# Weights of the second layer converted during the first and parked in DRAM, seven block products in its first group, and a sum kept in PSUM

## The chip, the cores and the metric

The kernel runs on one core of a Trainium2 chip. The metric is device time in microseconds (us) of one execution. Three runs of the kernel before took 1055.42, 1055.51 and 1057.75 us, so the median is 1055.51 us. Work is spread over TensorE (PE; PEld is its loading of weights), VectorE (DVE), ScalarE (ACT) and the DMA queue that SyncE (SP) feeds.

## The reference, cut to what matters

Attention between channels (its scores are 256 x 256), and then two feed-forward layers over 6016 tokens, 256 wide, with 2048 hidden features. The first layer has ELU between its two products, the second SiLU.

```python
def reference(...):
    attn_out = _attn_ref(**attn_kwargs)          # v @ softmax(kn^T qn / tau), (1, 6016, 256)
    x = attn_out.reshape(6016, 256)
    x = _moe_ref(x, w_in, w_out)                 # ELU
    return _moe2_ref(x, w_in2, w_out2)           # SiLU

def _moe_ref(x, w_in, w_out):
    h = x @ w_in                                 # 256 -> 2048
    g = np.where(h > 0.0, h, np.exp(np.minimum(h, 0.0)) - 1.0)
    return (g @ w_out).astype(np.float32)        # 2048 -> 256

def _moe2_ref(x, w_in, w_out):
    h = x @ w_in
    g = h * (1.0 / (1.0 + np.exp(-h)))
    return (g @ w_out).astype(np.float32)
```

## The kernel before, in words

The attention matrix is folded into the first layer's input weights (`m_group`), so that the two layers are the bulk. Tokens go in six groups of 1024 (the last has 896). `order` (line 642) lists twelve stretches, a layer and a group each: layer 1 on groups 0 to 5, then layer 2 on groups 0, 5, 1, 2, 3, 4. A stretch has eight steps j, one for each pair of 128 hidden features (16 pieces of 128 in all).

Every number in a product is carried as two float32r parts, a high and a low one, and a `product` (line 263) is three matmuls of up to 512 columns. `split` (line 259) makes the two parts: an ACT copy for the high one and a DVE subtraction for the low one.

The first product of a step is a 2 x 2 block product: two feature pieces by two halves of the tokens, over two halves of the 256 inputs. In a *plain* stretch (lines 648 and 740; here group 0 of both layers) it takes eight block products. In the others it takes seven, by sums of weight blocks (S1 to S4, `weight_sums`) and of inputs (T1 to T4, `x_made`). `first_a` (line 758) does four of them into the four PSUM banks x, y, w, z; ACT copies x to `u` in SBUF, and DVE adds u += y, v = w + u, v += z; v is the hidden value (1,1). `first_b` (line 777) lets three more products accumulate on x, w and z; x is the value (0,0), and DVE adds w + u and z + u give the other two in SBUF. So there are five adds a step. A `unit` (line 723) takes each hidden value through the activation: Relu and Exp on ACT and a scalar_tensor_tensor on DVE for ELU, two Silu on ACT for SiLU, and the split into `gs`. `second` (line 796) multiplies `gs` by the output weights `wo` into the four y banks.

The weights come as 64-bit numbers, and `convert` (line 378) makes two parts of them: load to a 4 KB buffer `st` (three in a ring), two ACT passes, two DVE tensor_scalar, a scalar_tensor_tensor and an integer add, and the split. The second layer's w2i also needs four 128x128 weight sums and a second split. Before the change, layer 2's weights are converted while layer 2's group 0 runs (lines 912 and 917), one piece of w2i and one of w2o in each of its eight steps, straight into `wa`, `a21` and `wo` that layer 1 has left by then. In this stretch only the four plain weight blocks are needed at once.

The order: all operations are recorded, and `in_order` (line 70) puts them out by a list schedule with the costs of line 36. PE's order is that of the program; ACT, DVE and SP get what is ready, the longest remaining way first. Engines then run their queues strictly in that order.

Of the kernel before, what the change touches and what calls it, by code (L numbers as in the profile page):

```python
# [11 lines left out]
F32 = mybir.dt.float32  # L12
F32R = mybir.dt.float32r
# [3 lines left out]
ALU = mybir.AluOpType  # L17
AX = mybir.AxisListType

P = 128  # L20
# [119 lines left out]
def channel_attention_elu_silu(  # L140
# [29 lines left out]
    _, N, C = q.shape  # L170
# [24 lines left out]
    small = one.tile([P, 224], F32, tag="small", name="small")  # L195
    wide = one.tile([P, GJ + 2 * MJ, C], F32, tag="wa", name="wide")
    v0 = wide[:, :GJ]
    wo = [one.tile([P, NF, C], F32R, tag=f"wo{a}", name=f"wo{a}") for a in range(2)]
    a21 = one.tile([P, 2, NP, P], F32R, tag="a21", name="a21")
    y_ps = [ps.tile([P, FC], F32, tag=f"y{i}", name=f"y{i}") for i in range(4)]  # L200
    h_ps = [ps.tile([P, FC], F32, tag=f"h{i}", name=f"h{i}") for i in range(4)]
    y_dram = [dram.tile([P, CT, GJ * P], F32, tag=f"yd{i}", name=f"yd{i}") for i in range(NG)]

    def f32(ap):
        return ap.bitcast(F32)
# [31 lines left out]
    def copy(out, src, **kw):  # L237
        act(out, src, AF.Copy, **kw)

    def tt(out, a, b, op):  # L240
        do("DVE", width(out.ap), lambda: nc.vector.tensor_tensor(at(out), at(a), at(b), op), [a, b], [out])  # L241
# [17 lines left out]
    def split(hi, lo, src):  # L259
        copy(hi, src)  # L260
        tt(lo, src, V(f32(hi.ap), hi.keys), ALU.subtract)
# [44 lines left out]
    def part(v, ap, *what):  # L306
        return V(ap, tuple(v.keys[0]._replace(what=x) for x in what))

    def cols_of(v, n):
        return V(v.ap[:, :n], v.keys)  # L310
# [15 lines left out]
    def wa_at(part, j, a):  # L326

        jj = range(j.start, j.stop) if isinstance(j, slice) else [j]
        aa = range(a.start, a.stop) if isinstance(a, slice) else [a]
        return V(wa[:, part, j, a], tuple(("wa", part, x, y) for x in jj for y in aa))  # L330

    def a21_at(part, j):
        jj = range(j.start, j.stop) if isinstance(j, slice) else [j]
        return V(a21[:, part, j], tuple(("a21", part, x) for x in jj))
# [21 lines left out]
    def load(name, i, *order):  # L356
        src = weights[name].rearrange("(t p) f -> p t f", p=P)
        src = src[:, :, 2 * i * HC : 2 * (i + 1) * HC] if name[-1] == "i" else src[:, 2 * i : 2 * i + 2]
        a, b = src.shape[1], src.shape[2]
        t = sts.take()  # L360
        words = t.ap.bitcast(I32)
        dma(V(words.rearrange("p (a b) -> p a b", a=a), t.keys + order), V(src, ()))
        words = words.rearrange("p (a b w) -> p a b w", a=a, w=2)
        src_of[name, i] = [part(t, words[:, :, :, w], w) for w in range(2)]

    def flat(ap):
        return ap.rearrange("p a b -> p (a b)")

    def weight_sums(s, w0, w1):

        get = lambda v, i: V(v.ap[:, :, i], v.keys)
        put = lambda i: part(s, s.ap[:, :, i], i)
        tt(put(0), get(w0, 1), get(w1, 1), ALU.add)
        tt(put(1), get(w0, 0), put(0), ALU.subtract)
        tt(put(2), get(w0, 0), get(w0, 1), ALU.subtract)
        tt(put(3), get(w1, 0), put(1), ALU.add)

    def convert(name, i, *order):
        load(name, i, *order)
        low, high = src_of.pop((name, i))  # L380
        t = cvs.take()
        a, b = low.ap.shape[1:3]
        w = V(t.ap.rearrange("p (a b) -> p a b", a=a), t.keys)
        wi = V(w.ap.bitcast(I32), t.keys)
        copy(w, V(f32(high.ap), high.keys), scale=2.0**-112)
        copy(low, V(low.ap.bitcast(U32), low.keys), scale=2.0**-29)
        ts(w, w, TOP, -TOP, ALU.min, ALU.max)
        ts(wi, wi, 3, None, ALU.logical_shift_left)
        stt(wi, V(high.ap, high.keys), SIGN, wi, ALU.bitwise_and, ALU.bitwise_or)
        tt(V(flat(wi.ap), wi.keys), V(flat(wi.ap), wi.keys), V(flat(low.ap), low.keys), ALU.add)  # L390
        if name == "w1i":
            s = slice(i % 2 * HC, (i % 2 + 1) * HC)
            hi, lo = (w1i_at(i // 2, a, slice(None)) for a in range(2))
            pieces = [(V(hi.ap[:, :, s], hi.keys), V(lo.ap[:, :, s], lo.keys), w)]
        elif name[-1] == "o":
            pieces = [(wo_at(0, i), wo_at(1, i), w)]
        else:
            pieces = [
                (wa_at(0, i, A11), wa_at(1, i, A11), V(w.ap[:, 0, :P], w.keys)),
                (a21_at(0, i), a21_at(1, i), V(w.ap[:, 0, P:], w.keys)),  # L400
                (
                    *(wa_at(a, i, slice(A12, A22 + 1)) for a in range(2)),
                    V(w.ap[:, 1].rearrange("p (a b) -> p a b", a=2), w.keys),
                ),
            ]
        for hi, _, src in pieces:
            copy(hi, src)
        for hi, lo, src in pieces:
            tt(lo, src, V(f32(hi.ap), hi.keys), ALU.subtract)
        if name == "w2i":  # L410
            h = hs.take()
            s = V(h.ap.rearrange("p (j a b) -> p j a b", j=1, a=4), h.keys)
            two = lambda c: V(w.ap[:, c].rearrange("p (j a b) -> p j a b", j=1, a=2), w.keys)
            weight_sums(s, two(0), two(1))
            split(*(wa_at(a, i, slice(S1, S4 + 1)) for a in range(2)), V(s.ap[:, 0], s.keys))

    with tc.manual_schedule():
        make_identity(nc, ident)
# [226 lines left out]
        def cols(n):  # L645
            return groups[order[n][1]][1] * P // 2

        def plain(n):

            return order[n][1] == 0  # L650

        base = [0] * len(order)
        for n in range(1, len(order)):
# [99 lines left out]
                )  # L753
            unit(s, u, ps)

        banks, us = {}, {}

        def first_a(s):
            n, j = steps[s]
            m = cols(n)  # L760
            if plain(n):
                for u in UNITS[:2]:
                    first_plain(s, u)
                return
            b = banks[s] = [cols_of(bank(), m) for _ in range(4)]
            for ps, a, o in zip(b, (A11, S2, S3, S1), (B11, T2, T3, T1)):
                product(ps, pair(j, a), x_at(n, o))
            x, y, w, z = b
            u, v = (cols_of(hs.take(), m) for _ in range(2))
            us[s] = u  # L770
            copy(u, x)
            tt(u, y, u, ALU.add)
            tt(v, w, u, ALU.add)
            tt(v, z, v, ALU.add)
            unit(s, (1, 1), v)

        def first_b(s):
            n, j = steps[s]
            if plain(n):
                for u in UNITS[2:]:  # L780
                    first_plain(s, u)
                return
            (x, _, w, z), u = banks.pop(s), us.pop(s)
            for ps, a, o in ((x, A12, B21), (w, A22, T4), (z, S4, B22)):
                product(ps, pair(j, a), x_at(n, o), start=False, skip_group_check=True)
            unit(s, (0, 0), x)
            t = cols_of(hs.take(), cols(n))
            tt(t, w, u, ALU.add)
            unit(s, (1, 0), t)
            tt(u, z, u, ALU.add)  # L790
            unit(s, (0, 1), u)


        final = len(order) - 1
# [107 lines left out]
        for s in range(len(steps) + 1):  # L902
            prev = s - 1
            now = s < len(steps)
            if now:
                n, j = steps[s]
                if n and j == 0:
                    x_made(n)
                if n == 0 and j % 2 and j < NP - 1:
                    convert("w1i", j + 1)  # L910
                    convert("w1i", j + 2)
                if order[n] == (2, 0):
                    convert("w2i", j)
                first_a(s)
            if s:
                chunk = f"w{order[steps[prev][0]][0]}o", steps[prev][1]
                if plain(steps[prev][0]) and chunk not in EARLY:
                    convert(*chunk)
                second(prev, (1, 1))
                if now:  # L920
                    second(prev, (1, 0))
            if now:
                if n == 0 and j % 2 and j < NP - 1:
                    m_group(j // 2 + 1)
                first_b(s)
            if s:
                second(prev, (0, 1))
                if not now:
                    y_store_final(1)
                    second(prev, (1, 0))  # L930
                second(prev, (0, 0))
                if steps[prev][1] == NP - 1:
                    if steps[prev][0] == final:
                        y_store_final(0)
                    else:
                        y_store(steps[prev][0])
# [36 lines left out]
```

## Time and profile before

| | |
|---|---|
| median of three runs | 1055.51 us |
| the profiled execution, first to last instruction | 1055.5 us |
| PE busy | 1042.7 us (99%) |
| DVE busy | 848.9 us (80%) |
| ACT busy | 716.0 us (68%) |
| granted TensorE clock, mean | 0.997 |
| DMA traffic | 54.60 MB |

The profiled execution has no time outside its span that the run's time would show: both are 1055.5. The first 62 us are the attention's scores; then come the twelve stretches, layer 1 from 62.7 us to about 560 us, layer 2 to 1050 us. An instruction's own time in a row is its latency; instructions of one engine overlap a little, so the distance from start to start (the pitch) is what one costs a full engine. Line numbers of the profile are those of the code above.

### The profile page before, as it was taken

Reading aid. Unit: us, or ns where it says so; the run is one execution under the profiler, and the core shown is the slowest. Engines: PE = TensorE matmul, PEld = TensorE weight load, DVE = VectorE, ACT = ScalarE, POOL = GpSimd, SP = SyncE. Lnnn points to the kernel's source line nnn. Section 1 sums busy time; section 2 is a strip of 40 time slices with the busy share of each in tenths; the row PEclk is TensorE's granted clock in tenths of the full one; section 3 lists DMA queues with packets and bytes.
Section 4 is the critical chain, followed back from the end, with each engine's and each line's share of the span. In section 5 each row is a group of like instructions: output and inputs, shape, how many; then the busy total and the mean of one; then the engine's idle time right before and its main releaser. Section 6 shows DMA issues by size and latency. Waiting matters only on the chain.

```text
span 1055.5 us, 13381 instructions
## 1 busy us (share of the span) xinstructions
PE 1042.7 (99%) x4848; PEld 882.5 (84%) x4848; DVE 848.9 (80%) x1432; ACT 716.0 (68%) x1304; POOL 0.8 (0%) x7
## 2 busy tenths in 40 slices
PE   8999999999999999999999999999999999999998
PEld 7778888888888888888998888998888888888997
DVE  6899999999989989989989966667668668657554
ACT  5699988786777777777879845555556455455543
POOL 0000000000000000000000000000000000000000
PEclk9999999999999999999999999999999999999999
DMA  9932241112003003002004303003003003001101
GB/s 348 286 94 60 81 98 62 41 21 60 1 6 74 1 1 75 1 1 80 20 1 140 110 1 75 6 1 76 1 1 80 0 1 80 1 1 23 18 1 40
DMA packets 99602, 54.60 MB, mean 52 GB/s; under 512 B 83024, under 2 KB 84304, under 8 KB 98896
## 3 DMA queue, kind: packets, MB, share of 16 engines
q1 hardware_dynamic: 99440, 53.49, 18.3%
q8 instruction: 38, 0.62, 0.2%
q10 hardware_dynamic: 96, 0.26, 0.1%
q14 instruction: 28, 0.23, 0.1%
HBM read 41.42 MB, written 12.32 MB: 51 GB/s over the span
## 4 chain that ended last, share of the span: by engine, by line
PE 93%; DMA 4%; DVE 1%; SPq 0%; ACT 0%; issue 0%; DVEq 0%
PE y L268 49%; PE h L268 44%; DMA ring<-in_q_dram 2%; DMA wide<-in_q_dram 1%; DMA wide<-in_v_dram 1%; DMA st<-in_moe_w_out_dram 0%; SPq L257 0%; DVE wo L241 0%; DVE cv L247 0%; DVE xs L241 0%; PE h L281 0%; DVE cv L241 0%; PE y L281 0%; PE h L276 0%; DVE cv L244 0%
## 5 line engine op out<-in xcount | busy, mean ns | idle before, releaser
L268 PE MATMUL y<-gs,wo 128*128 128x512 f32 (+1 forms) x2112 | 500.0, 386 | 0.7 <-DVE gs L241 0.7
L268 PE MATMUL h<-xs,wa 128*128 128x512 f32 (+1 forms) x1968 | 472.9, 386 | 0.0
L268 PEld LDWEIGHTS y<-gs,wo 128*128 128x128 f32 x2112 | 395.9, 188 | 76.2 <-DVE e L850 2.7
L268 PEld LDWEIGHTS h<-xs,wa 128*128 128x128 f32 x1968 | 368.0, 188 | 69.4 <-DVE h L241 2.0
L241 DVE TENSOR_TENSOR h<-h,h 128x512 f32<-128x512 f32 (+1 forms) x400 | 269.9, 675 | 78.5 <-PE h L268 69.1
L241 DVE TENSOR_TENSOR gs<-e,gs 128x512 fp32r<-128x512 f32 (+1 forms) x384 | 257.8, 677 | 71.0 <-ACT e L233 67.5
L233 ACT ACTIVATE e<-h 128x512 f32<-128x512 f32 (+2 forms) x385 | 229.8, 600 | 71.7 <-DVE h L241 48.3
L233 ACT ACTIVATE gs<-h 128x512 fp32r<-128x512 f32 (+1 forms) x192 | 117.0, 609 | 159.7 <-DVE h L241 109.8
L247 DVE SCALAR_TENSOR_TENSOR e<-e,h 128x512 f32<-128x512 f32 (+1 forms) x192 | 128.5, 676 | 26.2 <-ACT e L233 25.8
L233 ACT ACTIVATE gs<-e 128x512 fp32r<-128x512 f32 (+1 forms) x192 | 116.6, 614 | 23.0 <-DVE e L247 22.7
L233 ACT ACTIVATE e<-e 128x512 f32<-128x512 f32 (+1 forms) x192 | 117.2, 616 | 2.4
L233 ACT ACTIVATE h<-h 128x512 f32<-128x512 f32 (+1 forms) x80 | 46.3, 579 | 37.4 <-PE h L268 37.1
L241 DVE TENSOR_TENSOR xs<-big,xs 128x512 fp32r<-128x512 f32 (+1 forms) x74 | 48.7, 676 | 2.2 <-ACT xs L233 2.2
L268 PEld LDWEIGHTS y<-wo,gs 128*128 128x128 f32 x384 | 47.9, 192 | 1.1
L268 PE MATMUL y<-wo,gs 128*128 128x256 f32 x384 | 48.3, 283 | 0.0
L233 ACT ACTIVATE xs<-big 128x512 fp32r<-128x512 f32 (+1 forms) x74 | 43.1, 614 | 3.4 <-PE h L268 2.3
L241 DVE TENSOR_TENSOR sums<-sums 128x2048 f32<-128x2048 f32 (+2 forms) x16 | 28.7, 1792 | 10.4 <-ACT sums L233 10.2
L268 PE MATMUL h<-xs,a 128*128 128x512 f32 x96 | 27.3, 392 | 1.1 <-ACT a L233 1.1
L244 DVE TENSOR_SCALAR cv<-cv 128x512 f32<-128x512 f32 (+1 forms) x64 | 26.4, 430 | 1.3 <-ACT cv L233 1.3
L233 ACT ACTIVATE cv<-st 128x512 f32<-128x512 f32 x32 | 21.3, 671 | 7.6 <-DVE h L241 3.2
L276 PE MATMUL y<-ring 128*128 128x256 f32 x92 | 23.6, 415 | 1.7 <-DMA ring<-in_k_dram 1.7
L276 PEld LDWEIGHTS y<-ring 128*128 128x128 f32 x92 | 18.6, 207 | 5.7 <-issue 2.3
(84 smaller groups left out, 376.1 us busy)
## 6 DMA issues: line engine op xcount, KB each, us to landing
st<-in_moe_w_in_dram SPq DMA_DIRECT2D x16, 512.0 KB, 3.8
st<-in_moe_w_out_dram SPq DMA_DIRECT2D x16, 512.0 KB, 3.7
yd<-e SPq DMA_DIRECT2D x20, 256.0 KB, 2.5
big<-yd SPq DMA_DIRECT2D x5, 1024.0 KB, 4.7
out_dram<-big SPq DMA_DIRECT2D x38, 128.0 KB, 2.9
big<-in_v_dram SPq DMA_DIRECT2D x32, 128.0 KB, 3.4
wide<-in_q_dram SPq DMA_DIRECT2D x6, 512.0 KB, 10.0
wide<-in_k_dram SPq DMA_DIRECT2D x6, 512.0 KB, 10.7
```

The source lines that it names most:

```text
L233: nc.scalar.activation(at(out), at(src), func, **{k: at(x) for k, x in kw.items()}, **more)
L241: do("DVE", width(out.ap), lambda: nc.vector.tensor_tensor(at(out), at(a), at(b), op), [a, b], [out])
L244: do("DVE", width(out.ap) / 2, lambda: nc.vector.tensor_scalar(at(out), at(a), at(s1), at(s2), *op), [a, s1, s2], [out])
L247: emit = lambda: nc.vector.scalar_tensor_tensor(at(out), at(a), at(s), at(b), op0, op1)
L268: nc.tensor.matmul(at(out), at(lhs[a]), at(rhs[b]), start=start and a + b == 0, stop=stop and a == 1, **kw)
L276: emit = lambda: nc.tensor.matmul(at(out), at(lhs), at(rhs), start=start, stop=stop, **kw)
```

## The change

Three things. Layer 2's weights are converted by a new `put_by` in the steps of layer 1's groups 1 to 4 (four pieces in each group), each written to DRAM in its final two parts, sums of blocks included; `take_back` loads piece j into `wa` and `wo` when step j of layer 1's last group has read the old one. Then group 0 of layer 2 is no longer plain: `plain` is true for the first stretch alone. And `first_a` adds u to w and z in their PSUM banks before `first_b` accumulates on them, so that the three other values are read from PSUM; ACT makes a second copy (v from z), and DVE has four adds a step where it had five.

```diff
+    wo_both = one.tile([P, 2, NF, C], F32R, tag="wo", name="wo")
+    wo = [wo_both[:, a] for a in range(2)]
+    wa_dram = [dram.tile([P, 2, 7, P], F32, tag=f"wad{i}", name=f"wad{i}") for i in range(NP)]
+    wo_dram = [dram.tile([P, 2, 2, C], F32, tag=f"wod{i}", name=f"wod{i}") for i in range(NP)]
...
+    def put_by(name, i):
+        w, raw = in_f32(name, i)      # load, two ACT passes, four DVE operations, as in convert
+        wf = V(flat(w.ap), w.keys)
+        both = V(raw.ap.rearrange("p (a x) -> p a x", a=2), raw.keys)
...
+        split(half(both, 0), half(both, 1), wf)
+        if name == "w2o":
+            dma(V(wo_dram[i].rearrange("p a x r -> p a (x r)"), (("wod", i),)), both)
+            return
+        dma(V(wa_dram[i][:, :, A11], (("wad", i, 0),)), V(blocks(both)[:, :, 0], both.keys))
+        dma(V(wa_dram[i][:, :, A12 : A22 + 1], (("wad", i, 1),)), V(blocks(both)[:, :, 2:], both.keys))
+        t, more = cvs.take(), sts.take()
...
+        weight_sums(V(t.ap.rearrange("p (j a b) -> p j a b", j=1, a=4), t.keys), two(0), two(1))
+        both = V(more.ap.rearrange("p (a x) -> p a x", a=2), more.keys)
+        split(half(both, 0), half(both, 1), t)
+        dma(V(wa_dram[i][:, :, S1:], (("wad", i, 2),)), V(blocks(both), both.keys))
+
+    def take_back(name, i):
+        if name == "w2o":
+            keys = tuple(k for a in range(2) for k in wo_at(a, i).keys)
+            dma(V(f32(wo_both[:, :, 2 * i : 2 * i + 2]), keys), V(wo_dram[i], (("wod", i),)))
+        else:
+            keys = tuple(k for a in range(2) for k in wa_at(a, i, slice(0, 7)).keys)
+            dma(V(f32(wa[:, :, i]), keys), V(wa_dram[i], tuple(("wad", i, x) for x in range(3))))
...
         def plain(n):
-            return order[n][1] == 0
+            return n == 0
...
             u, v = (cols_of(hs.take(), m) for _ in range(2))
-            us[s] = u
             copy(u, x)
+            copy(v, z)
             tt(u, y, u, ALU.add)
-            tt(v, w, u, ALU.add)
-            tt(v, z, v, ALU.add)
+            tt(w, w, u, ALU.add)
+            tt(v, w, v, ALU.add)
+            tt(z, z, u, ALU.add)
             unit(s, (1, 1), v)
...
-            unit(s, (0, 0), x)
-            t = cols_of(hs.take(), cols(n))
-            tt(t, w, u, ALU.add)
-            unit(s, (1, 0), t)
-            tt(u, z, u, ALU.add)
-            unit(s, (0, 1), u)
+            for u, ps in zip(((0, 0), (1, 0), (0, 1)), (x, w, z)):
+                unit(s, u, ps)
...
-                if order[n] == (2, 0):
-                    convert("w2i", j)
+                if 0 < n < NG - 1 and j % 2 == 0:
+                    at_ = ((n - 1) * NP + j) // 2
+                    put_by(("w2i", "w2o")[at_ % 2], at_ // 2)
...
+                if steps[prev][0] == NG - 1:
+                    take_back("w2i", steps[prev][1])
+                    take_back("w2o", steps[prev][1])
```

PE's queue in layer 2, group 0: `y` are the banks of the second product, `h` those of the first, and a row's `x6` counts matmuls. A second product's half (12 matmuls) and the first product's second half that follows it, before:

```order
L268 MATMUL y2_72<-gs_291,wo0_67 128x512 x2
L268 MATMUL y2_72<-gs_291,wo1_68 128x512
L268 MATMUL y3_73<-gs_291,wo0_67 128x512 x2
L268 MATMUL y3_73<-gs_291,wo1_68 128x512
L268 MATMUL y0_70<-gs_291,wo0_67 128x512 x2
L268 MATMUL y0_70<-gs_291,wo1_68 128x512
L268 MATMUL y1_71<-gs_291,wo0_67 128x512 x2
L268 MATMUL y1_71<-gs_291,wo1_68 128x512
L268 MATMUL h2_76<-xs_345,a21_69 128x512 x3
L268 MATMUL h2_76<-xs_345,wa_376 128x512 x3
L268 MATMUL h3_77<-xs_345,a21_69 128x512 x3
L268 MATMUL h3_77<-xs_345,wa_376 128x512 x3
```

The same place of PE's queue now (lines are 3 higher, and the two parts of `wo` have one name):

```order
L271 MATMUL y2_71<-gs_306,wo_67 128x512 x3
L271 MATMUL y3_72<-gs_306,wo_67 128x512 x3
L271 MATMUL y0_69<-gs_306,wo_67 128x512 x3
L271 MATMUL y1_70<-gs_306,wo_67 128x512 x3
L271 MATMUL h2_75<-xs_360,wa_391 128x512 x3
L271 MATMUL h0_73<-xs_360,wa_391 128x512 x3
L271 MATMUL h1_74<-xs_360,wa_391 128x512 x3
```

The first product's half of 12 matmuls became one of 9; the other half keeps its 12, and the second product its 24.

DVE's queue in layer 1, group 2, from the fourth step's first add on (`h0_74` and `h1_75` are the banks w and z, `h1_97` is u, `h2_98` is v, `big` and `xs` belong to the next group's inputs), before:

```order
L241 TENSOR_TENSOR h1_97<-h3_77,h1_97 128x512
L247 SCALAR_TENSOR_TENSOR e2_94<-e2_94,h3_99 128x512
L241 TENSOR_TENSOR h2_98<-h0_74,h1_97 128x512
L241 TENSOR_TENSOR big0_84<-big1_85 128x512
L241 TENSOR_TENSOR h2_98<-h1_75,h2_98 128x512
L241 TENSOR_TENSOR gs_291<-e2_94,gs_291 128x512
L241 TENSOR_TENSOR xs_345<-big1_85,xs_345 128x512
L247 SCALAR_TENSOR_TENSOR e3_95<-e3_95,h2_98 128x512
L241 TENSOR_TENSOR h3_99<-h0_74,h1_97 128x512
L247 SCALAR_TENSOR_TENSOR e0_92<-e0_92,h2_76 128x512
L241 TENSOR_TENSOR h1_97<-h1_75,h1_97 128x512
```

The same step of DVE's queue now (`h0_73` and `h1_74` are w and z, `h0_111` is u, `h1_112` is v, `cv` and `st` are pieces of layer 2's weights):

```order
L244 TENSOR_TENSOR h0_111<-h3_76,h0_111 128x512
L244 TENSOR_TENSOR gs_306<-e2_109,gs_306 128x512
L244 TENSOR_TENSOR h0_73<-h0_73,h0_111 128x512
L244 TENSOR_TENSOR h1_74<-h1_74,h0_111 128x512
L244 TENSOR_TENSOR h1_112<-h0_73,h1_112 128x512
L244 TENSOR_TENSOR gs_306<-e0_107,gs_306 128x512
L244 TENSOR_TENSOR cv2_106<-cv1_105 128x128 x2
L244 TENSOR_TENSOR cv2_106<-cv1_105,cv2_106 128x128
L244 TENSOR_TENSOR st2_103<-cv1_105,st2_103 128x512
L250 SCALAR_TENSOR_TENSOR e3_110<-e3_110,h1_112 128x512
L244 TENSOR_TENSOR cv2_106<-cv1_105,cv2_106 128x128
L247 TENSOR_SCALAR cv0_104<-cv0_104 128x512
```

All four adds stand together near the step's head, w and z are written in place, and where the first list goes on with adds, conversions stand between v and the operation that reads it. DVE's queue has the conversions from the end of group 0 to the end of group 4 of layer 1, with some in every step.

## Rows read from the trace of the kernel before

**Rows 1.** The page, part 1: busy us, share, instructions.

```profile
PE 1042.7 (99%) x4848; PEld 882.5 (84%) x4848; DVE 848.9 (80%) x1432; ACT 716.0 (68%) x1304; POOL 0.8 (0%) x7
```

**Rows 2.** The page, part 2: tenths busy in 40 slices.

```profile
DVE  6899999999989989989989966667668668657554
...
PEclk9999999999999999999999999999999999999999
```

**Rows 3.** Windows: busy us (records) per engine, clock, DMA share, GB/s.

```profile
75.00:166.00 91.00, 91.00 (x404) 75.40 (x403) 90.95 (x166) 85.66 (x157) 0.00 (x0) 1.00 0.30 80
...
248.00:330.00 82.00, 82.00 (x361) 67.27 (x360) 74.33 (x120) 61.74 (x114) 0.00 (x0) 1.00 0.12 26
...
560.00:647.00 87.00, 87.00 (x389) 72.64 (x388) 70.00 (x152) 61.52 (x126) 0.00 (x0) 1.00 0.28 88
807.00:889.00 82.00, 82.00 (x363) 67.91 (x363) 56.82 (x89) 44.75 (x80) 0.00 (x0) 1.00 0.11 26
```

**Rows 4.** Chain of waits in time order: start us, us, what.

```profile
248.83 2.99 PE y L268 x12
251.83 2.20 PE h L268 x9
254.03 2.75 PE y L268 x12
...
588.21 2.72 PE h L268 x12
```

**Rows 5.** Lines of DVE, 248 to 330 us, shapes apart.

```profile
L241 DVE TENSOR_TENSOR h<-h,h 128x512 f32<-128x512 f32 x40 | 27.4, 686 | 1.6 <-PE h L268 1.2
...
L251 DVE STREAM_TRANSPOSE big<-big 128x1024 f32<-128x1024 f32 x2 | 2.5, 1238 | 0.0
```

**Rows 6.** Timeline of DVE, four places: start us, us, instruction.

```profile
84.42 0.68 DVE L241 CUSTOM_DVE_ANT_0 cv<-st,cv 128x1024 uint16<-128x1024 uint16 x1
85.02 0.69 DVE L241 TENSOR_TENSOR gs<-e,gs 128x512 fp32r<-128x512 f32 x1
85.62 0.69 DVE L247 SCALAR_TENSOR_TENSOR cv<-st,cv 128x512 int32<-128x512 int32 x1
...
90.76 0.43 DVE L244 TENSOR_SCALAR cv<-cv 128x512 f32<-128x512 f32 x1
91.09 1.25 DVE L251 STREAM_TRANSPOSE big<-big 128x1024 f32<-128x1024 f32 x1
...
261.16 0.69 DVE L241 TENSOR_TENSOR h<-h,h 128x512 f32<-128x512 f32 x1
261.76 0.69 DVE L241 TENSOR_TENSOR big<-big 128x512 f32<-128x512 f32 x1
...
562.21 0.28 DVE L241 TENSOR_TENSOR h<-cv,h 128x128 f32<-128x128 f32 x1
562.41 0.69 DVE L247 SCALAR_TENSOR_TENSOR cv<-st,cv 128x512 int32<-128x512 int32 x1
```

**Rows 7.** Timeline of a step, 288 to 294 us, ACT, DVE and PE.

```profile
288.20 0.58 ACT L233 ACTIVATE h<-h 128x512 f32<-128x512 f32 x1
...
289.02 1.48 DVE L241 TENSOR_TENSOR h<-h,h 128x512 f32<-128x512 f32 x2
...
291.01 0.68 DVE L241 TENSOR_TENSOR h<-h,h 128x512 f32<-128x512 f32 x1
293.06 0.69 DVE L247 SCALAR_TENSOR_TENSOR e<-e,h 128x512 f32<-128x512 f32 x1 [1.36 <-ACT e L233]
...
292.66 2.20 PE L268 MATMUL h<-xs,wa 128*128 128x512 f32 x9
```

**Rows 8.** Waits, and DMA issues with KB and us to landing.

```profile
ACT cv L233 <- DMA st<-in_moe_w_out_dram: 2.3, 2, 1.3
...
st<-in_moe_w_out_dram SPq DMA_DIRECT2D x16, 512.0 KB, 3.7
big<-yd SPq DMA_DIRECT2D x5, 1024.0 KB, 4.7
```

More of the change, by code (lines that the diff above doesn't have):

```diff
@@ L197, in channel_attention_elu_silu @@
     v0 = wide[:, :GJ]
-    wo = [one.tile([P, NF, C], F32R, tag=f"wo{a}", name=f"wo{a}") for a in range(2)]
+    wo_both = one.tile([P, 2, NF, C], F32R, tag="wo", name="wo")
+    wo = [wo_both[:, a] for a in range(2)]
     a21 = one.tile([P, 2, NP, P], F32R, tag="a21", name="a21")
@@ L364, in load @@
         src_of[name, i] = [part(t, words[:, :, :, w], w) for w in range(2)]
+        return t
     def flat(ap):
@@ L376, in weight_sums, with in_f32 @@
         tt(put(3), get(w1, 0), put(1), ALU.add)
-    def convert(name, i, *order):
-        load(name, i, *order)
+    def in_f32(name, i, *order):
+        raw = load(name, i, *order)
         low, high = src_of.pop((name, i))
@@ L390, in convert @@
         tt(V(flat(wi.ap), wi.keys), V(flat(wi.ap), wi.keys), V(flat(low.ap), low.keys), ALU.add)
+        return w, raw
+    def convert(name, i, *order):
+        w, _ = in_f32(name, i, *order)
         if name == "w1i":
@@ L394, in convert @@
             pieces = [(V(hi.ap[:, :, s], hi.keys), V(lo.ap[:, :, s], lo.keys), w)]
-        elif name[-1] == "o":
+        else:
             pieces = [(wo_at(0, i), wo_at(1, i), w)]
[L397 to L405, printed above, removed]
         for hi, _, src in pieces:
@@ L409, in convert @@
             tt(lo, src, V(f32(hi.ap), hi.keys), ALU.subtract)
[L410 to L415, printed above, removed]
+    def put_by(name, i):
+        w, raw = in_f32(name, i)
+        wf = V(flat(w.ap), w.keys)
+        both = V(raw.ap.rearrange("p (a x) -> p a x", a=2), raw.keys)
+        half = lambda v, a: V(v.ap[:, a].bitcast(F32R), v.keys)
+        blocks = lambda v: v.ap.rearrange("p a (x r) -> p a x r", r=P)
+        split(half(both, 0), half(both, 1), wf)
[5 more added lines that the diff above has]
+        t, more = cvs.take(), sts.take()
+        two = lambda c: V(w.ap[:, c].rearrange("p (j a b) -> p j a b", j=1, a=2), w.keys)
+        weight_sums(V(t.ap.rearrange("p (j a b) -> p j a b", j=1, a=4), t.keys), two(0), two(1))
[6 more added lines that the diff above has]
+            dma(V(f32(wo_both[:, :, 2 * i : 2 * i + 2]), keys), V(wo_dram[i], (("wod", i),)))
+        else:
+            keys = tuple(k for a in range(2) for k in wa_at(a, i, slice(0, 7)).keys)
+            dma(V(f32(wa[:, :, i]), keys), V(wa_dram[i], tuple(("wad", i, x) for x in range(3))))
     with tc.manual_schedule():
@@ L754, in first_plain @@
             unit(s, u, ps)
-        banks, us = {}, {}
+        banks = {}
         def first_a(s):
@@ L782, in first_b @@
                 return
-            (x, _, w, z), u = banks.pop(s), us.pop(s)
+            x, _, w, z = banks.pop(s)
             for ps, a, o in ((x, A12, B21), (w, A22, T4), (z, S4, B22)):
                 product(ps, pair(j, a), x_at(n, o), start=False, skip_group_check=True)
-            unit(s, (0, 0), x)
-            t = cols_of(hs.take(), cols(n))
-            tt(t, w, u, ALU.add)
-            unit(s, (1, 0), t)
-            tt(u, z, u, ALU.add)
-            unit(s, (0, 1), u)
+            for u, ps in zip(((0, 0), (1, 0), (0, 1)), (x, w, z)):
+                unit(s, u, ps)
         final = len(order) - 1
@@ L916, in channel_attention_elu_silu @@
                 chunk = f"w{order[steps[prev][0]][0]}o", steps[prev][1]
-                if plain(steps[prev][0]) and chunk not in EARLY:
+                if steps[prev][0] == 0 and chunk not in EARLY:
                     convert(*chunk)
```

## The prediction

> **What bounds the kernel now.** I read the page's busy times and slices first, then windows by stage, the chain of waits in time order, and DVE's lines and timeline where it is full. PE is busy for 1042.7 of 1055.5 us, at full clock in every slice [rows 1, 2]. In each of the four windows PE is busy for the whole window [rows 3]. The chain runs along PE from the first stretch to the last, twelve matmuls of 512 columns in 2.72 us, so 2.72 / 12 = 0.227 us each [rows 4]. So a matmul that is left out is worth 0.227 us, wherever nobody else becomes the last to be waited for. The little that PE loses is at the seams between stretches: the chain's pieces there are 2.99 for 2.72, 2.20 for 2.04 and 2.75 for 2.72 us, 0.46 us in all at 248 us [rows 4].
>
> DVE is the second to look at. It is nearly full in layer 1 and has room in layer 2: 90.95 of 91.00 us in group 0, 74.33 of 82.00 in group 2, 70.0 of 87.0 in layer 2's group 0, 56.82 of 82.00 in an ordinary stretch of layer 2 [rows 3]. The change takes work of PE and DVE out of layer 2 and puts DVE work into layer 1. So the question is whether layer 1 has room for it.
>
> **The matmuls removed.** Layer 2's group 0 has eight steps, and each goes from eight block products of three matmuls to seven: 8 x 3 = 24 fewer matmuls of 512 columns, 24 x 0.227 = 5.44 us. The whole stretch before is 8 x 48 x 0.227 = 87.0 us, which is the window at 560 us, full of PE [rows 3]. After, it is 8 x 45 x 0.227 = 81.6 us, as the window at 807 us, where seven-product steps of the same layer run with DVE at 56.82 and ACT at 44.75 of 82.00 us and PE without a gap [rows 3]. The conversions leave this stretch, and what comes in (seven input blocks instead of four, the adds) is what the later stretches already have. So I count the 5.44 us in full there.
>
> The new weights for it come back from DRAM during layer 1's last group. Piece j is issued when step j has read the old one and is wanted about eight steps later, 8 x 45 x 0.227 x 448 / 512 = 71 us; 1 MB from DRAM lands after 4.7 us [rows 8]. That is hidden, and stays hidden at ten times the price. On SP's queue there are 48 more issues, and the inputs of the next group stand behind some of them; those are wanted for the first time a stretch later, so I count nothing.
>
> **The DVE work put into layer 1.** What one DVE operation costs a full DVE is the distance from start to start: 0.60 us for 512 columns with two tensors, also for the integer add of the conversion and for an add that reads PSUM (261.16 to 261.76), 0.33 for a tensor_scalar, 0.20 for a weight sum of 128 columns [rows 6]. In group 2's window there are 120 operations, two of them transposes of 2.5 us together [rows 3, 5]: 118 x 0.60 + 2.5 = 73.3 us of the 82.0.
> - One add a step goes: 8 x 0.60 = 4.8 us less.
> - A w2o piece is 2 x 0.33 + 3 x 0.60 = 2.46 us. A w2i piece has four sums and a second split on top, 2.46 + 4 x 0.20 + 0.60 = 3.86 us. Two of each in a group: 12.6 us more.
> - Sum: 73.3 - 4.8 + 12.6 = 81.1 of 82.0 us. DVE is left 0.9 us a group, in groups 1 to 4.
>
> That it can run so full without PE noticing is shown by group 0: 90.95 of 91.00 us with conversions between the urgent operations, and PE full for the same 91.00 us [rows 3]. But that is one plain stretch, without the adds that stand between a step's first products and its last, and now four groups of the other kind follow. At a seam PE loses 0.46 us before [rows 4]; DVE then had 82.00 - 74.33 = 7.7 us of idle time in the group to catch up, and now 0.9. I add 0.3 us for each of the five seams that follow, 1.5 us, as the likeliest price, between 0 and about 4 us (two more seams' worth at each).
>
> **The edits with no price of their own.** ACT gets eight copies of 0.58 us a group [rows 7] and 14 operations of the four conversions, at the same 0.58 us 8.1 us more: 61.74 + 4.6 + 8.1 = 74.5 of 82.0, 91%. In group 0 it ran 85.66 of 91.00, 94%, beside a full PE [rows 3].
>
> The in-place adds add a wait: the product on w must now follow u, w and v, that on z also its own add. Before, the third add of a step ended at 291.01 + 0.68 = 291.69, while the three products began at 292.66, that on w at 292.66 + 0.68 = 293.34 and that on z at 294.02 [rows 7]. One more add of 0.60 ends at 292.3, 1.0 us before w's product, even if all four had to be done. Its cover is that one microsecond; without it PE waits inside `first_b`, and the product on z and twelve matmuls of the second product stand behind. In the other direction the banks w and z stay taken until Relu, Exp and DVE's operation have read them. x has to go through the same before, comes first and gets its bank back first, so w and z have 0.68 and 1.36 us more than it has.
>
> What the trace of before has no row for is DVE writing PSUM, 16 times a group. It is not below the 0.60 us of an add that reads PSUM, and at most the whole 0.69 us of its latency [rows 6]: 0 to 16 x 0.09 = 1.4 us a group. I take 0, since DVE's reading of PSUM showed no extra. The Trainium skill says otherwise ("Perfetto Trace Analysis", section Optimizing Scalar/DVE Operations): DVE has some 60 ns of overhead on SBUF and 125 ns on PSUM. For reading, the trace does not agree, since 0.60 us holds for both [rows 6]; for writing no row shows it. By that page's 65 ns the 16 writes would be 1.0 us a group, an estimate, which would just use up what DVE has left.
>
> **Sum.** The profiled execution's span is 1055.5 us, which is also the median of the three runs (1055.51). 1055.5 - 5.4 + 1.5 = 1051.6 us.
>
> **Rivals.**
> - *The converted pieces come late.* A piece's buffer must be stored, then loaded again, 3.7 us for the load alone [rows 8], with three buffers in the ring; ACT's and DVE's queues hold urgent work behind the operation that waits for it. For it: before, two loads held ACT up for 2.3 us in all, 1.3 at most [rows 8]. Against: that was two of 16, and DVE in group 0 had no idle time from it. If a quarter of the 16 pieces are late by 1.15 us, 4.6 us come on top of the sum without the seams' 1.5: 1055.5 - 5.4 + 4.6 = 1054.7, no change that can be told.
> - *Operands in PSUM cost DVE more.* The 16 in-place adds and the 16 scalar_tensor_tensor of a group that now read PSUM at up to 0.09 us extra are 2.9 us, 2.0 over what is left, four times: 1055.5 - 5.4 + 8.0 = 1058.1. Against it stands the add that read PSUM at 0.60. This is the mechanism of the page above.
> - *DVE is overfull* (slower). To the 1.4 us of the writes come operations that read what the one just before them wrote: of such a pair the second started 1.48 - 0.68 = 0.80 us after the first, not 0.60 [rows 7]. Two a step are 16 x 0.20 = 3.2 us a group. Then DVE lacks 1.4 + 3.2 - 0.9 = 3.7 us in each of four groups, and PE waits for all of it: 1055.5 - 5.4 + 14.8 = 1064.9. It decides from about 2.2 us a group on (5.4 + 3.2 over four). For it: such pairs are there before. Against: DVE's order now has a filler between most of them, and in group 0, full as it was, no such idle time is left.
>
> **Chances.** My forecast has 0.55, late pieces 0.21, PSUM operands 0.10, an overfull DVE 0.14. About 0.3%, 3.2 us, is what a measurement of this kernel can tell from no change. So faster has 0.55, no change 0.31, slower 0.14. The forecast's own range is 1049.8 (the seams cost nothing more, and a little of what they cost is won back) to about 1054. The range of 8 in 10 takes in the two cases of no change: 1049.8 to 1059.
>
> **What would show it.** Right: layer 2's group 0 takes 81.6 us in place of 87.0; in layer 1 a group takes 81.6 to 82.3 us, with DVE at 98% or more of it, and PE's gaps are still at the seams. Late pieces: ACT or DVE waits for `st` or `wad` landings, several of a microsecond. PSUM operands: the pitch of the adds onto w and z is over 0.60 us. Overfull: PE waits for DVE in the middle of groups 1 to 4, and a group takes 84 us or more. The prediction is wrong altogether if PE waits in layer 2's group 0 for weights from DRAM.

## The result and the profile after

The changed kernel takes 1062.58 us (median of five runs, 1061.03 to 1068.34) beside 1055.51 us for the one before: a ratio of 1.0074, 95% interval [1.0057, 1.0091]. It is slower by 7.1 us, where I had forecast 1051.6 us, 3.9 us faster, and a range of 1049.8 to 1059.

First what came as the sum had it. The page's part 1 of the changed kernel (busy us, share, instructions) answers to [rows 1]:

```profile
PE 1040.4 (98%) x4824; PEld 875.5 (83%) x4824; DVE 826.3 (78%) x1375; ACT 746.3 (70%) x1387; POOL 0.9 (0%) x7
```

The reader is to see 24 matmuls fewer (4848 before) and no engine busier but ACT. The windows of after (busy us and records of PE, PEld, DVE, ACT, POOL; clock; DMA share; GB/s) tell where, beside [rows 3]:

```profile
75.00:166.00 91.00, 90.63 (x399) 74.22 (x398) 90.00 (x164) 84.09 (x152) 0.00 (x0) 1.00 0.25 63
166.00:248.00 82.00, 78.57 (x336) 62.06 (x336) 76.13 (x135) 67.79 (x129) 0.00 (x0) 1.00 0.36 106
248.00:330.00 82.00, 78.97 (x343) 63.41 (x342) 77.67 (x136) 67.94 (x130) 0.00 (x0) 1.00 0.23 68
330.00:412.00 82.00, 81.88 (x361) 67.19 (x361) 80.69 (x140) 71.12 (x136) 0.00 (x0) 1.00 0.30 87
...
560.00:647.00 87.00, 87.00 (x392) 73.03 (x390) 58.16 (x92) 55.72 (x106) 0.00 (x0) 1.00 0.12 44
```

Layer 2 is full of PE. Layer 1's groups 1 and 2 (the windows from 166 and from 248 us) lose 3.4 and 3.0 us of PE, and DVE isn't full there: 76.13 and 77.67 us, with more room than in group 3's window (80.69), where PE loses 0.1. So it does not look like too much work. From the first product of a stretch to that of the next, groups 1 to 4 of layer 1 take 87.8, 87.1, 82.2 and 83.2 us, where each took 82.0 to 82.1 before; layer 2's group 0 takes 81.1 in place of 86.5. Two cuts through the same traces give the size. From the first product of layer 1 to the end is 999.0 us after (60.25 to 1059.25) and 992.8 before (62.71 to 1055.53), 6.2 more. And the gaps between neighbouring matmuls, start to start less 0.227 us for 512 columns, those over 0.05 us, come to 13.9 us after and 2.9 before, all of them before 565 us: -5.4 + 11.0 = 5.6 us.

Who is waited for stands in the waits of after (us in total, times, longest), beside [rows 8], where `cv` had two waits of 2.3 us for one of these loads, and two of 1.9 us for the other:

```profile
ACT cv L236 <- DMA st<-in_moe_w_in_dram: 11.8, 10, 3.8
PEld h L271 <- DVE e L250: 9.6, 11, 3.1
ACT cv L236 <- DMA st<-in_moe_w_out_dram: 7.2, 5, 2.5
```

ACT waits 19.0 us in 15 waits for loads of weights, up to 3.8 us at a time. The first three of them, 1.5 us, are for layer 1's own pieces; the other 12, 17.5 us, are for layer 2's. One of these places, read from SP to PE; first SP's timeline (start us, us, instruction):

```profile
223.90 0.34 SPq L260 DMA_DIRECT2D wod<-st  x1
226.51 0.37 SPq L260 DMA_DIRECT2D st<-in_moe_w_out_dram  x1
226.98 1.18 SPq L260 DMA_DIRECT2D wad<-st  x2
231.48 0.37 SPq L260 DMA_DIRECT2D st<-in_moe_w_in_dram  x1
```

Twice a load into a buffer stands right behind the store that empties it, and twice SP waits until that store has landed: from 223.90 to 226.51, and from the end of the stores' issue (228.16) to 231.48. In the whole run 15 loads of layer 2's pieces follow a store of their buffer, and 14 of them go out within 0.1 us of that store's landing, 2.2 to 4.1 us after it was issued. Then the chain of waits (start, us, what):

```profile
227.54 3.87 DMA wad<-st
...
231.48 3.57 DMA st<-in_moe_w_in_dram
...
236.81 3.01 ACT e L236 x6
```

And the three engines there:

```profile
235.07 0.67 ACT L236 ACTIVATE cv<-st 128x512 f32<-128x512 f32 x1 [2.50 <-DMA st<-in_moe_w_in_dram]
...
238.33 1.89 DVE L250 SCALAR_TENSOR_TENSOR e<-e,h 128x512 f32<-128x512 f32 x3 [2.27 <-ACT e L236]
...
239.07 2.34 PE L271 MATMUL h<-xs,wa 128*128 128x512 f32 x9 [1.86 <-DVE e L250]
```

The store (128 KB) takes 3.87 us, the load behind it 3.57. ACT stands for 2.50 us at the first operation on a piece that is wanted 300 us later, with the urgent Exp operations behind it; DVE then has nothing for 2.27 us, and PE loses 1.86. The same at 312 us costs PE 2.8.

### The profile page after: what moved, and what is told of

Read it like the earlier page. It is cut to its first block, busy times and chain, and to the rows that moved or that the text cites. A ratio compares the mean times of both kernels' runs of the same rounds, so it can differ in the third digit from the quotient of the medians.

```text
span 1059.2 us, 13497 instructions
## 1 busy us (share of the span) xinstructions
PE 1040.4 (98%) x4824; PEld 875.5 (83%) x4824; DVE 826.3 (78%) x1375; ACT 746.3 (70%) x1387; POOL 0.9 (0%) x7
## 4 chain that ended last, share of the span: by engine, by line
PE 74%; DVE 11%; ACT 7%; DMA 5%; issue 3%; SPq 0%; DVEq 0%; ACTq 0%
PE y L271 37%; PE h L271 33%; ACT e L236 4%; PE y L279 4%; DVE h L244 3%; DVE gs L244 2%; DVE e L250 2%; DMA st<-in_moe_w_in_dram 2%; DMA wad<-st 1%; ACT gs L236 1%; DVE cv L244 1%; ACT xs L236 1%; DVE cv L250 0%; DVE st L244 0%; DVE cv L247 0%
## 5 line engine op out<-in xcount | busy, mean ns | idle before, releaser
L271 PE MATMUL h<-xs,wa 128*128 128x512 f32 (+1 forms) x1992 | 480.0, 386 | 6.5 <-DVE e L250 5.5
L244 DVE TENSOR_TENSOR gs<-e,gs 128x512 fp32r<-128x512 f32 (+1 forms) x384 | 255.0, 675 | 95.4 <-ACT e L236 93.2
L244 DVE TENSOR_TENSOR h<-h,h 128x512 f32<-128x512 f32 (+1 forms) x352 | 228.7, 678 | 79.3 <-PE h L271 56.7
L236 ACT ACTIVATE e<-h 128x512 f32<-128x512 f32 (+2 forms) x385 | 226.2, 599 | 51.3 <-DVE h L244 47.4
L236 ACT ACTIVATE h<-h 128x512 f32<-128x512 f32 (+1 forms) x176 | 103.7, 589 | 135.0 <-PE h L271 134.8
L236 ACT ACTIVATE gs<-h 128x512 fp32r<-128x512 f32 (+1 forms) x192 | 116.4, 607 | 74.5 <-DVE h L244 40.3
L250 DVE SCALAR_TENSOR_TENSOR e<-e,h 128x512 f32<-128x512 f32 (+1 forms) x192 | 124.2, 670 | 19.3 <-ACT e L236 18.7
L236 ACT ACTIVATE e<-e 128x512 f32<-128x512 f32 (+1 forms) x192 | 113.9, 622 | 1.5
L236 ACT ACTIVATE gs<-e 128x512 fp32r<-128x512 f32 (+1 forms) x192 | 113.1, 625 | 0.6 <-DVE e L250 0.4
L250 DVE SCALAR_TENSOR_TENSOR cv<-st,cv 128x512 int32<-128x512 int32 x32 | 21.8, 685 | 0.2
```

The source lines that it names most:

```text
L236: nc.scalar.activation(at(out), at(src), func, **{k: at(x) for k, x in kw.items()}, **more)
L250: emit = lambda: nc.vector.scalar_tensor_tensor(at(out), at(a), at(s), at(b), op0, op1)
L271: nc.tensor.matmul(at(out), at(lhs[a]), at(rhs[b]), start=start and a + b == 0, stop=stop and a == 1, **kw)
```

## The experiments

All were timed in five rounds beside runs of the kernel before (median 1055.21 for e1 to e8, 1055.5 for the rest). In the table, *layers* is the time from layer 1's first product to the end, *gaps* are PE's over 0.05 us, *ACT* is what it waits for the loads of `st`; 1.1 to 4.6 us of that is for layer 1's own pieces, in every kernel. These three come from the one profiled execution of each kernel: e16's took 1059.59 us, 4.2 more than its median, the others are within 2.2 us of theirs. The expectations count gaps a little lower (12.0 for the changed kernel, 6.9): that count took a few of 0.23 and 0.45 us for matmuls missing from the trace, but none is missing.

| kernel | us | ratio to before, 95% | layers | gaps | ACT |
|---|---|---|---|---|---|
| before | 1055.51 | | 992.8 | 2.9 | 4.9 |
| after | 1062.58 | 1.0074 [1.0057, 1.0091] | 999.0 | 13.9 | 19.4 |
| e1 | 1054.95 | 0.9996 [0.9987, 1.0005] | 991.9 | 7.2 | 11.5 |
| e2 | 1050.24 | 0.9951 [0.9938, 0.9965] | 987.8 | 3.4 | 3.2 |
| e3 | 1055.76 | 1.0006 [0.9998, 1.0015] | 993.5 | 3.6 | 4.7 |
| e4 | 1059.61 | 1.0036 [1.0024, 1.0049] | 995.9 | 11.0 | 16.1 |
| e5 | 1057.75 | 1.0025 [1.0015, 1.0034] | 995.4 | 10.8 | 6.3 |
| e6 | 1052.56 | 0.9974 [0.9964, 0.9984] | 990.9 | 6.1 | 7.8 |
| e7 | 1054.43 | 0.9992 [0.9983, 1.0001] | 991.3 | 6.5 | 8.9 |
| e8 | 1062.78 | 1.0076 [1.0062, 1.0089] | 999.7 | 14.6 | 18.1 |
| e9 | 1063.53 | 1.0071 [1.0059, 1.0084] | 1000.7 | 15.2 | 21.8 |
| e10 | 1051.46 | 0.9962 [0.9950, 0.9975] | 989.2 | 4.6 | 7.6 |
| e11 | 1053.26 | 0.9979 [0.9969, 0.9989] | 991.3 | 6.6 | 2.7 |
| e12 | 1052.21 | 0.9971 [0.9959, 0.9982] | 989.6 | 4.6 | 5.3 |
| e13 | 1051.99 | 0.9968 [0.9956, 0.9980] | 989.4 | 4.7 | 3.9 |
| e14 | 1062.24 | 1.0067 [1.0055, 1.0079] | 1001.2 | 16.2 | 17.9 |
| e15 | 1050.16 | 0.9950 [0.9937, 0.9963] | 988.3 | 3.7 | 2.5 |
| e16 | 1055.40 | 1.0003 [0.9993, 1.0014] | 995.1 | 8.5 | 13.3 |

### Which part of the change costs: e1 to e4

e1: the schedule reckons the stores' landing 2.5 us later.

```diff
         fixed, each, late, own = COST[engine]
+        late += more          # 2.5 for the four stores in put_by, else 0
```

> The changed kernel, but its list schedule is told that a converted piece's store lands 2.5 us later than it assumed, so that it puts the next piece's operations later in the queues; nothing else is edited. Theory 1 (a piece's reload lands after ACT's queue has come to the operation that reads it, ACT stops, DVE and PE follow): the 19.0 us that ACT waits for landings in st fall under 5, PE's gaps from 12 us to 5 or less, about 1055 us. Theory 2 (DVE has too little room in layer 1, whatever the transfers do): no change, 1061 to 1064 us.

e2: no `put_by`, no `take_back`. Left out is the conversion of layer 2's weights; layer 2 computes with those of layer 1.

```diff
-                    put_by(("w2i", "w2o")[at_ % 2], at_ // 2)
...
-                    take_back("w2i", steps[prev][1])
-                    take_back("w2o", steps[prev][1])
```

> The changed kernel without put_by and take_back: layer 2 is computed with layer 1's weights that are still in wa and wo, so no piece is converted, stored or loaded. Seven products in layer 2's group 0 and the adds in PSUM stay. Theories 1 and 2 both: only the 24 matmuls are gone, 5.4 us under the kernel before, 1050 us, with PE's gaps at 3 us as before. Theory 3 (the adds in PSUM themselves cost, by w's product waiting for one more add and by banks held until the activation has read them): PE's gaps stay at 8 us or more, 1055 to 1058 us.

e3: the kernel before with the adds in PSUM banks and nothing else.

```diff
+            copy(v, z)
             tt(u, y, u, ALU.add)
-            tt(v, w, u, ALU.add)
-            tt(v, z, v, ALU.add)
+            tt(w, w, u, ALU.add)
+            tt(v, w, v, ALU.add)
+            tt(z, z, u, ALU.add)
```

> The kernel before with the adds in PSUM alone; weights converted where they were, eight products in layer 2's group 0. Theories 1 and 2: DVE has 4.8 us a group more room and nothing is added, 1055.5 us within 1.5. Theory 3: slower in every stretch with seven products, over 1059 us.

e4: the changed kernel with the five adds of before.

```diff
-            tt(z, z, u, ALU.add)
...
+            t = cols_of(hs.take(), cols(n))
+            tt(t, w, u, ALU.add)
+            tt(u, z, u, ALU.add)
```

> The changed kernel with the five adds a step of before (into SBUF), the rest as changed. DVE then has 8 x 0.60 = 4.8 us a group more to do in groups 1 to 4, 85.9 us by the sum of pitches in a group of 82. Theory 2: PE waits for all that is too much, 3.9 us a group, some 15 us over the changed kernel, about 1078 us. Theory 1: the schedule puts what does not fit into group 5, and lateness is what counts, within 4 us of 1062.6 us.

e2 settles the first term: without the conversion the kernel is 5.0 us faster than before, so the 24 matmuls are worth what they were counted at, and the adds in PSUM cost nothing; e3 says the latter by itself. e4 puts one add a step more on DVE and is 3 us faster than the changed kernel, not 15 slower: DVE's fullness doesn't decide. And e1 takes 7.6 us out with the same instructions in another order. So what costs is the place of the pieces in the order. I took e1's figure for proof of its reason; that was too soon, as the next two groups show.

### Queue, buffers, or the order: e5 to e8

e5 and e8 are e1 with another number (6.0 and -1.5 us).

> Stores reckoned 6 us late in place of 2.5; the instructions are the same, only their order differs. Theory A (the written order counts on the stored pieces' buffers too early; 2.5 us took out 7.6 us of the loss): what ACT still waits for landings of the pieces' buffers in e1 (5.4 + 3.5 + 2.6 us) goes to under 3 us, PE's gaps fall from 6.9 to between 3.4 (the sum without any conversion) and 5, and the time to 1051 to 1053.5 us. Rival B (what is left in e1 is DVE being 97 to 98% full in groups 1 to 4): waits for landings fall and PE's gaps don't, 1054 to 1056.

> Stores reckoned 1.5 us earlier than in the changed kernel, the opposite of e1. Theory A: the order counts on buffers 1.5 us sooner still, ACT's waits for landings grow from 21 us to 27 or more, PE's gaps from 12 to 15 or more, 1064 to 1070 us. Rival C (e1 won because any other order happens to be better than the changed kernel's): 1055 to 1062, no order by size.

e6: the stores on GpSimd's queue.

```diff
+    "POOL": (0.37, 0, 2.3, 0.0),
...
+        dma(..., by="POOL")       # the four stores in put_by
```

> As the changed kernel, but the four kinds of stores of converted pieces are issued on GpSimd's queue, which has nothing else to do, at the cost that the order reckoned with before; loads and everything else stay on SP. Theory A1 (SP works strictly in order, and a load that waits for a buffer holds the next piece's stores up: 1.3 us at 226 to 227 us in the changed kernel): ACT's waits for landings drop by a third or more from 21 us, PE's gaps from 12 to about 7, 1055 to 1059 us. Rival A2 (the landings themselves, 3.9 us for the store and 3.6 for the load that follows, are what the order counts on too early, SP only passes it on): as the changed kernel, 1060 to 1063.

e7: four buffers for the pieces.

```diff
-        ... Ring("st", 3, 4096), ... Ring("h", 5, 2048)
+        ... Ring("st", 4, 4096), ... Ring("h", 4, 2048)
```

> As the changed kernel with four buffers in the ring of pieces in place of three; the memory for it comes from the ring h (four in place of five) and from an unused part of one small tile. Theory A with the ring as its cause (a load stands right behind the store of the same buffer): with one more buffer the load need not wait, ACT waits for landings under 8 us in place of 21, PE's gaps fall from 12 to 5 to 7, 1053 to 1057. If the order only fills DVE's room sooner, or the ring h was the tighter one (waits of ACT or DVE for h grow): 1059 to 1064.

e5 goes against e1's reading: 6.0 us is worse than 2.5. e8 is no test of it: with -1.5 the schedule writes the same order as for the changed kernel, operation for operation on every engine, so its 1062.78 us is that kernel measured again. e5's waits for `st` did fall, to 6.3 us, but one new gap of 4.6 us came at 499.8 us: a piece was pushed into layer 1's last group, where the weights come back. Its waits from 494 to 506 us name the transfer:

```profile
ACT e L237 <- DMA yd<-e: 6.7, 2, 5.0
DVE e L251 <- ACT e L237: 5.9, 2, 5.5
```

(a store of 256 KB took 6.3 us there, 3.1 in the median of the changed kernel.) e7, with a fourth buffer, is 8.2 us faster than the changed kernel, within the 1053 to 1057 us expected of the ring; but its order is another one too. e6 beats before, by more than either of its theories gave. By its expectation SP's single file would be the cause; but e6 moved the order as well.

### The same order on either queue: e9 to e12

e9 keeps the changed kernel's order and issues the stores on GpSimd's queue; e10 keeps e6's order and issues them on SP.

```diff
 e9:
+        queue = nc.gpsimd if by == "POOL" else queue
 e10, against e6:
-        "POOL": (nc.gpsimd, "POOL")
+        "POOL": (nc.sync, "POOL")
```

> ACT's, DVE's and PE's order are word for word those of the changed kernel; only the queue that issues the stores of converted pieces is GpSimd's. Theory A1 (SP's single file passes every late buffer on to the pieces behind it): the waits of ACT for landings fall from 21 us to under 10, PE's gaps from 12 to 5 to 8, 1053 to 1057 us. Rival D (e6 won because the order came out otherwise when the stores were reckoned on a queue of their own): 1060 to 1063 us, waits as in the changed kernel.

> The counterpart: ACT's, DVE's and PE's order of e6, but the stores issued by SP, at the places that e6's reckoning gives them. Theory A1: the waits come back, ACT waits over 12 us for landings, 1056 to 1062 us. Rival D: as e6, 1051.5 to 1053.5 us.

e11 is e6 with 2.5 us more for the stores (as e1), e12 is e6 with e7's buffers.

> e6 with the stores also reckoned 2.5 us later. What is left in e6 is 7.8 us of ACT's waits for landings and 5.9 us of PE's gaps, 2.4 over the kernel without conversions. Theory A with both halves (single file and reckoned landing): waits under 4 us, 1050.5 to 1052.5. If a later piece only runs into the next group's transfers, as in e5: 1053 to 1056.

> e6 with four buffers for the pieces (and four in the ring h). If a load behind a store of its own buffer is what is left in e6: waits under 4 us, 1050.5 to 1052.5. If the two edits pay for the same waits: as e6, 1052 to 1053.5; if the smaller ring h costs: above that, with waits for h.

The single file falls: e9 is as slow as the changed kernel, e10 as fast as e6. e12 is level with e6, which by its expectation says that the fourth buffer and e6's edit win the same time. e11 has short waits for `st` (2.7 us) and is no faster than e6: here, too, a store of `yd` at the start of layer 1's last group takes 5.9 us, and PE has a gap of 1.5 us at 500.1 us. The timelines of SP and GpSimd in e9:

```profile
230.53 0.37 SPq L261 DMA_DIRECT2D st<-in_moe_w_out_dram  x1
...
227.52 0.55 POOL L261 DMA_DIRECT2D wod<-st  x1 [10.20 <-ACT e L236]
```

The load comes 3.0 us after its store although SP issues nothing in between. The landing is what takes the time, on whichever queue. The Trainium skill has both halves ("DMA: Bandwidth & Descriptors"): its section Two DMAs through the same engine are not ordered says that a dependent transfer has to wait for the first one's completion, and that the same queue is no substitute for it; its section Issuing engines are not separate DMA queues says that several issuing engines save only the time of issuing. This case agrees with both: the load came 2.61 us after its store on one queue (223.90 to 226.51) and 3.01 on two, and two queues won nothing (e9).

What e6's order has and the changed kernel's hasn't is then in the reckoning that writes the order, and it stands in two lines of the code:

```
"SP": (0.37, 0, 2.3, 0.0),        # fixed, each, late, own
...
return a.cost + (a.own if a.engine == b.engine else a.late)
```

Between two operations of one engine the plan counts `own`, and for SP that is 0.0: behind a store's own cost on SP (0.4 to 1.5 us by its size) a load into the same buffer may follow at once. Only toward other engines are 2.3 us counted for landing. By the plan's own list 15 loads of converted pieces follow a store of their buffer in the changed kernel, 13 of them at 0.0 us; in e6 and e10, where the stores count as another engine, the least is 2.3. (It also explains why e8 changed nothing: its number went into `late`, as e1's did, which no load on SP looks at. The users of those buffers on other engines have 13 us or more in the plan. e1 only gave the pieces a longer remaining way, and so other places in the order; that it won 7.6 us by this is a fact, why just those places are better I did not test.)

### One number: e13 to e16

e13 gives the four stores an `own` of 2.3 us, and nothing else; e15 4.0, e16 1.15. e14 keeps e10's queue for the stores in the plan and takes the landing before SP's loads out.

```diff
 e13, e15, e16:
+        own += landing            # 2.3, 4.0, 1.15 for the four stores in put_by
 e14, against e10:
-        return a.cost + (a.own if a.engine == b.engine else a.late)
+        return a.cost + (a.own if a.engine == b.engine or a.engine + b.engine == "POOLSP" else a.late)
```

> The changed kernel, stores on SP, with one number other: between a store of a converted piece and the load into the same buffer, both on SP, the reckoning that writes the order now counts 2.3 us for the landing; before it counted nothing between two transfers of SP. Theory E (that nothing is what made the order bad: loads and the first operation on them were set 2.3 to 3.6 us too early): ACT's waits for landings under 10 us, PE's gaps 4 to 6.5, 1051 to 1053.5 us, as e10. Rival F (e10 won because the reckoning saw SP free of the stores' 0.4 to 1.5 us each): 1058 to 1063 us.

> The counterpart of e10: the reckoning has a queue of its own for the stores, but counts no landing between a store and SP's load into the same buffer. Theory E: as the changed kernel, 1060 to 1064 us, ACT's waits for landings about 20 us. Rival F: as e10, 1051 to 1053 us.

> As e13 with 4.0 us for the landing. The slowest reload in the changed kernel came 3.9 us after its store was issued. Theory E: the waits for landings go down further, to under 5 us; with no more pieces than before in the last group, 1050.5 to 1053 us. If pieces are pushed back into the stretch from 494 us, where the weights come back from DRAM (as in e5): 1053 to 1057.

> As e13 with half the landing, 1.15 us. Theory E, by size: between the changed kernel and e13 in ACT's waits (10 to 18 us) and in time, 1054 to 1060 us. If any other order does as well: no place between the two.

The time follows the number: 1062.6 us at 0, 1055.4 at 1.15, 1052.0 at 2.3, 1050.2 at 4.0, and ACT's waits for layer 2's pieces go from 17.5 us to 9.9, 2.1 and 0.8. e14, which differs from e10 in this alone, goes back to 1062.2 with ACT's long waits:

```profile
ACT cv L237 <- DMA st<-in_moe_w_in_dram: 13.3, 9, 4.1
PEld h L272 <- DVE e L251: 10.1, 8, 3.8
```

In e15 the waits are gone; most of what is left is for layer 1's pieces:

```profile
ACT cv L237 <- DMA st<-in_moe_w_in_dram: 1.2, 3, 0.6
...
ACT cv L237 <- DMA st<-in_moe_w_out_dram: 0.9, 1, 0.9
```

At the place read above (SP, then ACT, in e15's timeline) SP waits for the landing too, 2.66 us from the store to the load; but ACT comes to the piece 7.5 us after the load's issue, and waits no more:

```profile
220.34 0.34 SPq L261 DMA_DIRECT2D wod<-st  x1
220.90 0.52 SPq L261 DMA_DIRECT2D wad<-st  x1
223.00 0.37 SPq L261 DMA_DIRECT2D st<-in_moe_w_out_dram  x1
...
230.51 0.68 ACT L237 ACTIVATE cv<-st 128x512 f32<-128x512 f32 x1
```

And its windows of groups 1 and 2 show PE full, and DVE fuller than in the changed kernel:

```profile
166.00:248.00 82.00, 81.68 (x358) 66.57 (x357) 79.40 (x138) 71.55 (x137) 0.00 (x0) 1.00 0.30 86
248.00:330.00 82.00, 81.89 (x361) 67.42 (x361) 81.26 (x145) 70.80 (x136) 0.00 (x0) 1.00 0.31 89
```

e15 is the best version: 5.3 us faster than before and 12.4 faster than the changed kernel, with the same instructions on the same queues as the latter. It is level with e2, which does no conversion at all: with its order put right, putting the weights by costs nothing that these runs can tell.

## Why the prediction was wrong

- **The 24 matmuls, 5.44 us: right.** e2 gives 5.0, e15 5.3. Layer 2 has no gap in the changed kernel, and the weights' way back from DRAM is hidden, as said.
- **DVE's room, 81.1 of 82.0 us: right, and harmless.** e15 has 81.26 in group 2's window, and PE loses 0.1 us there. The 1.5 us for the seams were too much: e15's gaps are 0.8 us over before. ACT's 74.5 us were too many, 70.80 in e15: 0.58 us is a copy's latency, its pitch is 0.48.
- **Adds in PSUM at no price: right.** In e13's full DVE the adds, some of which write PSUM, keep their pitch; three of them take 270.28 - 268.49 = 1.79 us, and operations on a value in PSUM follow at 0.60 too:

```profile
268.49 1.88 DVE L245 TENSOR_TENSOR h<-h,h 128x512 f32<-128x512 f32 x3
270.28 0.68 DVE L245 TENSOR_TENSOR st<-cv,st 128x512 fp32r<-128x512 f32 x1
...
273.88 1.28 DVE L251 SCALAR_TENSOR_TENSOR e<-e,h 128x512 f32<-128x512 f32 x2
275.09 0.69 DVE L245 TENSOR_TENSOR gs<-e,gs 128x512 fp32r<-128x512 f32 x1
```

  So the rivals on PSUM operands and on an overfull DVE fell. The latter's 1064.9 us is the forecast nearest to the 1062.6, and its sign came true, two groups of over 84 us with PE waiting for DVE; but DVE was itself waiting for ACT, and e15 has it fuller without loss. That it came near is luck.
- **"On SP's queue there are 48 more issues ... I count nothing": this is the step that failed.** I looked at the inputs behind the stores, not at the loads behind them that need the store's buffer. Such a pair costs the landing, 2.6 to 3.9 us from issue to issue at the place read above; the plan counts the store's own 0.4 to 1.5 us and 0.0 for the landing. In place of nothing, ACT waited 17.5 us for layer 2's pieces, all but 0.8 of it for such loads, and PE's gaps grew by 11.0 us, of which 10.2 are gone in e15.
- **The rival of late pieces had the mechanism and the wrong size.** It said a quarter of 16 pieces, 1.15 us each, 4.6 us. There were 12 waits of ACT for these pieces, 17.5 us, up to 3.8 each, and PE lost 11.0 us more than before. Its price came from two loads of before, where no load in the ring follows a store [rows 8]; both waits lie ahead of layer 1, at 46.8 and 50.4 us, where none of its steps stand behind them. So those rows could not bound it from above. A rough bound was to be had from rows: 15 pairs by a load's landing of 3.7 us is 55 us, far above the range. And the argument against it, that group 0 runs full with no idle time, was about conversions without stores.
- **The base.** I took the profiled execution (span 1055.5) to be the median run. A run's time is 1.8 us over its span in these runs (1061.03 beside 1059.2 for the profiled one of after, 1050.28 beside 1048.5 for e15), so that execution was about 1.8 us above the median; its layer 1 began at 62.71 us, late among those seen later. As only differences were added, the forecast would not have moved; but spans of two profiled executions must not be subtracted.

## What to carry to other kernels

When a change puts a store and a reload into a ring of buffers, look up what the schedule counts between the two: on one queue the landing has to be waited out as on two (2.61 and 3.01 us here). An operation in the background costs what stands behind it in its engine's queue, so bound its lateness by the count of its transfers times their landing, not by the waits of a kernel that had no such pair. And an edit that wins is no proof of its reason: e1 won 7.6 us by a number that the loads never see, and only the same order on another queue, and then one number in four sizes, told the causes apart. Look, too, whether an edit of a schedule's number changes the order at all: e8's did not.

## What the hardware showed unexpectedly

- The part before layer 1 does not always take the same time. Layer 1's first product starts at 60.0 to 62.8 us in the eighteen profiled executions of the table. ACT, DVE and SP do the same there in the same order in all but e7 and e12; before and e3 have the same operations on PE as well, and start at 62.71 and 60.46 us. What makes the difference stays open. The start in before, and in e13, the earliest:

```profile
62.71 1.11 PE L268 MATMUL h<-xs,a 128*128 128x512 f32 x3 [1.08 <-ACT a L233]
```

```profile
60.00 1.11 PE L272 MATMUL h<-xs,a 128*128 128x512 f32 x3 [1.11 <-ACT a L237]
```

- A store of 512 KB from SBUF lands sooner than a load of 512 KB, in the median. The issues of after (KB, us to landing):

```profile
st<-in_moe_w_in_dram SPq DMA_DIRECT2D x16, 512.0 KB, 3.7
...
wad<-st SPq DMA_DIRECT2D x8, 512.0 KB, 3.0
wod<-st SPq DMA_DIRECT2D x8, 512.0 KB, 2.6
...
wad<-st SPq DMA_DIRECT2D x8, 256.0 KB, 2.4
wad<-st SPq DMA_DIRECT2D x8, 128.0 KB, 2.2
```

  A quarter of the bytes saves only 0.8 us, so by these figures most of it is a fixed part, an estimate. But single ones take far longer: the 128 KB store at 227.54 took 3.87 us and the one at 302.36 took 4.05, each with a load of 512 KB under way beside it; the one at 203.96, with none, took 2.18. That may be why 4.0 us was a better number to plan with than 2.3; no run tests it.
